# Three filter products and four tail-round blocks on Pool, with new orders of the filter stage and of the early inverse

## The chip, the cores and the metric

One core of a Trainium2 chip. The metric is the time of one execution on the device in microseconds (us); less is better. TensorE (PE) multiplies matrices and writes PSUM; VectorE (DVE), ScalarE (ACT) and GpSimd (POOL) do the element work; SyncE (SP) issues most transfers.

## The reference

`x` is 2048 x 576 in bfloat16.

```
h   = x + irfft2(rfft2(layernorm(x)) * (w_r + 1j*w_i))            # filter: 2048 x 289 complex weights
out = h + (gelu(layernorm(h) @ w_gate) * (layernorm(h) @ w_up)) @ w_down   # 576 -> 4608 -> 576
```

## The kernel before

The two-dimensional transforms are written as matmuls with tables. The kernel runs in stages: layer norm and a first transform over 128 rows (to about 20 us of the span), the **filter stage** (20 to 47 us), the **early inverse** with the second layer norm of the first six row tiles (47 to 58 us), and then the gated network in four blocks of 512 rows, 36 tiles of hidden columns each, every block followed by its down product. The inverse of the other ten row tiles is slipped into the first down product.

**Filter stage.** The 2048 row frequencies are cut into 16 groups i = 0..15. Each group goes through steps that are written as words, and the stage is a list of such words, `SEQF` (line 29). A word is a letter, a group and, if need be, an engine: `A` ACT (the default for evacuations), `D` DVE, `P` POOL, `x` for "directly from PSUM".

- `D i` and `d i` (`st_D`, line 621; matmuls on L628): the transform over columns, six matmuls in `D`, four in `d`, and then an evacuation of 128x576 from PSUM to the SBUF tile CUS.
- `B q` (`st_B`, line 635; L641): 16 matmuls, for groups 2q and 2q+1, which need both groups' CUS.
- `b i` (`ev_B`, line 644): evacuation of 128x576 from PSUM to YS, which has two buffers, i mod 2. With `x` there is none.
- `T i` (`st_T`, line 649; L653): the filter product, 128x1152, of YS (or, with `x`, of PSUM) with the weights WS in SBUF, into TP. On DVE before.
- `V i` (`st_V`, line 655; L661): 16 matmuls back from TP, and an evacuation of 128x512 to V.
- `Z i` (`st_Z`, line 666): copies the last 32 columns of each part of TP, 128x128, to ZR, where up to four groups lie beside one another.
- `R q` (`st_R`, line 670; L676 and L680): the **tail rounds**, eight matmuls over the four groups in ZR, and two products on DVE that spread the result with a mask MK into its block form VR. R0 serves group 0, R1 to R3 four groups each, R4 three.

All plain evacuations and copies go through one helper, `ev` (line 617), and so show as line L618. The program keeps the order of the words on each engine: an engine works its own words in the order of the list, and waits for others by semaphores. PSUM has eight banks, used as four pairs; `take` (line 600) gives a `D`, a `V`, an `R` or one of the two groups of a `B` the pair that was free for longest. A matmul that gets a used pair waits for the evacuation of what lay there. POOL operations wait for the POOL operation before.

**Early inverse.** `SEQ` (line 30) is a second list of words: `I` inverse over columns (L761; the first matmuls read V, the last VR), `N` inverse over rows and the residual add on DVE (L804, L821), `s` or `S` the squares for the layer norm on ACT or DVE, `q` and `c` root and reciprocal, `n` and `e` the scaling on DVE and POOL, `z` and `D` the transposes, `g` and `h` the first tiles of the gate and up products, for half of the rows each.

Of the kernel before, what the change touches and what calls it, by code (L numbers as in the profile page):

```python
# [4 lines left out]
BF16 = mybir.dt.bfloat16  # L5
F32 = mybir.dt.float32
ACTF = mybir.ActivationFunctionType
ALU = mybir.AluOpType
# [4 lines left out]
NP = 6  # L13
# [12 lines left out]
LORD = "x0-2 x2-4 a0-4 x4-8 a4-8 x8-12 x12-16 a8-16".split()  # L26
SPLIT = tuple(int(w[1:-1]) for w in SEQ1 if w[0] == "F")
ACT_TILES = tuple(int(w[1:]) for w in SEQ1 if w[0] == "Q")
SEQF = """D1 D0 d1D d0 D3 D2 d3 B0 b0 b1D T1 d2 D4 T0 d4 D5 B1 D6 b2 d5 b3D d6 T3 Z0D V1 Z1P T2 B2 D7 b4 D8 b5 d7D d8 T4 V3 V0 B3 T5 b6 b7 V2 D10 Z2P Z3D Z4D D9 d10 d9 T6 D11 T7 Z5P R0 d11 R1 B4 D13 Z6P b8 T8 b9 Z7D d13 T9 B5 D12 b10 b11 Z8D V4D V5 d12 Z9P T10 R2 D14 D15 d14 V9 d15 Z10P B6 T11 b13D b12 V7 V6 T13 V8 B7 T12 b15 V10 b14x T14x Z11P V11 T15 Z12P V12 V13 Z13P Z14P R3 V14 V15 Z15P R4""".split()
SEQ = """I0 I1 N0 I2 N1 s0 I3 S1 N2 q0 c0 I4 n0 s2 e0 q1 N3 e1 n1 I5 c1 z0 s3 e2 n2 D1 N4 q2 c2 D2 n3 N5 g10 e3 g00 h10 z3 h00 g20 g11 h20 h11 g01 g21 h01 h21""".split()  # L30
QR0 = ((0, 2), (2, 3), (3, 4))
QR = QR0 + ((4, NPRE), (NPRE, 8), (8, 16))
DSTEP, DLAG, ALAG = 288 // (16 - NPRE), 24, 26
# [293 lines left out]
def _build(nc, A_x, A_w_r, A_w_i, B_w_gate, B_w_up, B_w_down, out):  # L327
    P = Prog(nc)
    T = build_tables()
    dram = {n: nc.inline_tensor(_np_bf16(T[n]), name="c_" + n.lower()) for n in T}  # L330
    PE, DVE, ACT, SP, POOL = "pe", "dve", "act", "sp", "pool"
# [3 lines left out]
    sb = SbufMap(nc, base, top)  # L335
# [12 lines left out]
    V = sb.alloc("V", [128, 4, NT, NG, 8], BF16)  # L348
    VR = sb.alloc("VR", [128, NT, 2, NG, 8], BF16)
# [27 lines left out]
    MK = sb.alloc("MK", [128, 4], F32)  # L377
# [30 lines left out]
    TP = sb.alloc("TP", [128, NP, 2, 2, KW], BF16)  # L408
    ZR = sb.alloc("ZR", [128, 3, 4, 4, 32], BF16)
    GS = sb.alloc("GS", [128, 2, 2, KW], BF16)  # L410
    sb.off = v_off
    AT = sb.alloc("AT", [128, 36, 512], BF16)
    HT1 = sb.alloc("HT1", [128, 5, 512], BF16)
# [6 lines left out]
    PS = nc.alloc_psum_tensor("PS", [128, 4096], F32)  # L420

    def bank(b, p0=0, p1=128, c0=0, c1=512):
        return PS[p0:p1, b * 512 + c0:b * 512 + c1]

    def banks(b, n, w):
        return PS[:, b * 512:(b + n) * 512].rearrange("p (a c) -> p a c", a=n)[:, :, 0:w]
# [20 lines left out]
    for i, w in enumerate(LORD):  # L447
        c0, c1 = (int(v) for v in w[1:].rstrip("@").split("-"))
# [4 lines left out]
    WP = ((0, 4), (4, 10), (10, 16))  # L453
# [19 lines left out]
    wkeys = [[("W", pl, j, i) for pl in range(2) for i in range(6 if j else 7)] for j in range(3)]  # L473
# [106 lines left out]
    for w in SEQ1:  # L580
        a = w[1:]
# [4 lines left out]
    while c < NT:  # L586
        c1 = c + 1
        while c not in ACT_TILES and c1 < NT and c1 not in ACT_TILES:
            c1 += 1
        src, f, keys = (SA[:, 0, c:c1], -1.0 / D, "SA0") if c in ACT_TILES else (MV1[:, c:c1, 0], -1.0, "MV1")  # L590
        P.op(POOL, lambda g, c=c, c1=c1, src=src, f=f: g.tensor_scalar(NM[:, c:c1], src, f, 1.0, op0=ALU.mult, op1=ALU.mult),
             r=[(keys, k) for k in range(c, c1)], w=[("NM", k) for k in range(c, c1)])
# [5 lines left out]
    FB, used, held = {}, [0] * 4, {}  # L598
# [5 lines left out]

    for t, w in enumerate(SEQF):
        k, i, a = w[0], int(w[1:].rstrip("ADPx")), w[-1]
# [10 lines left out]
    def ev(eng, dst, src, r, w):  # L617
        fn = (lambda v: v.tensor_copy(dst, src)) if eng != ACT else (lambda a: a.activation(dst, src, ACTF.Copy))  # L618
        P.op(eng, fn, r=r, w=w)

    def st_D(i, second=False, eng=ACT):
        b0, s3 = FB["D", i], i % 4
        for j in range(3 - second):
            for half in range(2):
                o = half ^ second
                us, h0, b = (1 - o, 3 - o, 4)[j], 64 * half, b0 + o
                aft = [d_done[i, o]] if second and j == 0 else []
                d_done[i, o] = P.op(PE, lambda t, b=b, us=us, h0=h0, o=o, s=(not second and j == 0), e=(second and j == 1): t.matmul(  # L628
                    bank(b, 0, 128, 0, 2 * HK), U[h0:h0 + 64, us, i, :, :, :].rearrange("p s n e -> p (s n e)"), FT[h0:h0 + 64, 4 if us == 4 else 2 * o + us // 2, :], start=s, stop=e),
                    r=[("U", q, us, i // 8) for q in range(len(GROUPS))] + ["FT"], w=[("PS", b)], after=aft)  # L630
        if second:
            ev(eng, CUS[:, s3, :, :].rearrange("p a (j r) -> p a j r", r=2), banks(b0, 2, 2 * HK).rearrange("p r (a j) -> p a j r", a=2),
               [("PS", b0), ("PS", b0 + 1)], [("CU", s3)])
# [12 lines left out]
        if eng is not None:  # L646
            ev(eng, YS[:, i % 2, :, :], banks(b0, 2, KW), [("PS", b0), ("PS", b0 + 1)], [("Y", i % 2)])

    def st_T(i, direct=False):
        w4 = WS[:, :, i, 1:K2].unsqueeze(1).to_broadcast([128, 2, 2, KW])  # L650
        y, rk = (banks(FB["B", i], 2, KW), [("PS", FB["B", i] + h) for h in range(2)]) if direct else (YS[:, i % 2, :, :], [("Y", i % 2)])
        y4 = y.unsqueeze(2).to_broadcast([128, 2, 2, KW])
        P.op(DVE, lambda v: v.tensor_tensor(TP[:, i % NP, :, :, :], y4, w4, op=ALU.mult), r=rk + wkeys[sum(i >= w[1] for w in WP)], w=[("T", i % NP)])  # L653

    def st_V(i, b, eng):
        sp_ = int(i == 0)
# [10 lines left out]
        q, j = ((i - 1) // 4 % 2, (i - 1) % 4) if i else (2, 0)  # L667
        ev(eng, ZR[:, q, :, j, :], TP[:, i % NP, :, :, 256:KW].rearrange("p h w k -> p (h w) k"), [("T", i % NP)], [("ZR", q, j)])

    def st_R(q, b):  # L670
        j0, j1 = (4 * q - 3, min(4 * q + 1, NG)) if q else (0, 1)
        n, sp_, zb = j1 - j0, int(q == 0), (q - 1) % 2 if q else 2
        for k in range(4):
            for h in range(2):
                h0, vt = 64 * h, (0, 1, 1, 2)[k]
                P.op(PE, lambda t, k=k, h=h, h0=h0, vt=vt: t.matmul(bank(b + h, 0, 128, 0, 128), ZR[h0:h0 + 64, zb, k, :, :].rearrange("p a k -> p (a k)"),  # L676
                                                                    VT[h0:h0 + 64, sp_, vt, :].rearrange("p (k n e) -> p n k e", k=2, n=16), start=(k == 0), stop=(k == 3)),
                     r=[("ZR", zb, j) for j in range(4)] + ["VT"], w=[("PS", b + h)])
        for h in range(2):
            P.op(DVE, lambda v, h=h: v.tensor_tensor(VR[:, :, :, j0:j1, 4 * h:4 * h + 4].rearrange("p n k g e -> p (n k) g e"),  # L680
                                                     bank(b + h, 0, 128, 0, 128).rearrange("p (a e) -> p a e", e=4).unsqueeze(2).to_broadcast([128, 32, n, 4]),
                                                     MK[:, 0:n].unsqueeze(1).unsqueeze(3).to_broadcast([128, 32, n, 4]), op=ALU.mult),
                 r=[("PS", b + h), "MK"], w=[("V", g, 2) for g in range(j0, j1)])

    def idle_ft(n, b):
        for _ in range(n):
# [3 lines left out]
    d_done = {}  # L690
    for w in SEQF:
        i, e = int(w[1:].rstrip("ADPx")), {"A": ACT, "D": DVE, "P": POOL, "x": None}.get(w[-1], ACT)
        if w[0] == "D":
            st_D(i)
        elif w[0] == "d":
            st_D(i, True, e)
        elif w[0] == "B":
            st_B(i)
        elif w[0] == "b":
            ev_B(i, e)  # L700
        elif w[0] == "T":
            st_T(i, w[-1] == "x")
        elif w[0] == "Z":
            st_Z(i, e)
        elif w[0] == "V":
            st_V(i, FB["V", i], e)
        elif w[0] == "R":
            st_R(i, FB["R", i])


    wdv = B_w_down[:, :].rearrange("(c p) d -> p c d", p=128)
# [30 lines left out]

    MT = [int(w[1:]) for w in SEQ if w[0] == "M"]
    SLOT, last = {}, [0] * 4
    held = {}
    for t, w in enumerate(SEQ):
        k, i = w[0], int(w[1:])
        if k in "IJNMADzg":
            b = min((b for b in range(4) if b not in held), key=lambda b: last[b])
# [14 lines left out]
    def i_ev(c, eng=ACT):  # L764
        sl, b0 = c % 2, SLOT["I", c]
        if c == 0:
            P.op(DVE, lambda v, sl=sl, b0=b0: v.tensor_copy(GS[:, sl, 0, 0:KW], bank(b0, 0, 128, 0, KW)), r=[("PS", b0)], w=[("G", sl, 0)])
            P.op(ACT, lambda a, sl=sl, b0=b0: a.activation(GS[:, sl, 1, 0:KW], bank(b0 + 1, 0, 128, 0, KW), ACTF.Copy), r=[("PS", b0 + 1)], w=[("G", sl, 1)])
        else:
            ev(eng, GS[:, sl, :, 0:KW], banks(b0, 2, KW), [("PS", b0), ("PS", b0 + 1)], [("G", sl, 0), ("G", sl, 1)])  # L770

# [26 lines left out]
    def st_N(c):  # L798
        sl = c % 2
        for h in range(2):  # L800
            b = SLOT["N", c] + h
            for i in range(2):
                rhs = GS[:, sl, i, ::-1] if h else GS[:, sl, i, :]
                P.op(PE, lambda t, b=b, h=h, i=i, c=c, rhs=rhs: t.matmul(bank(b, 0, 128, 0, 288), IT[:, h * i, c, :], rhs, start=(i == 0 and c not in MT), stop=(i == 1)),  # L804
# [147 lines left out]

    gu_early = sorted({int(w[1]) for w in SEQ if w[0] == "g"})
    assert gu_early == list(range(len(gu_early)))
# [6 lines left out]
    st_I01()  # L961
    for w in SEQ[2:]:
        RUN[w[0]](int(w[1:]))
# [4 lines left out]


    fdead = ["DT", "IT", "J0", "J1", "ZD"] + [(n_, c) for n_ in ("ATB", "ATS") for c in range(NT)] + [("G", 0, 0), ("G", 0, 1), ("G", 1, 0), ("G", 1, 1), ("Y", 0), ("Y", 1)]  # L970
    fdead += [("T", a) for a in range(NP)] + [("ZR", a, h) for a in range(2) for h in range(4)]
    fnew = ([("AT", f) for f in range(36) if f not in gu_early] + [("GL", 0), ("GL", 1)] + [("HT", 1, i, k) for i in range(4) for k in range(5)])


# [5 lines left out]
    for j, c in enumerate(DEFS):  # L980
        b = 4 + 2 * (c % 2)
# [92 lines left out]
```

## Time and profile before

| | us |
|---|---|
| median of 3 runs | 489.96 (489.91 to 490.04) |
| the profiled execution | 489.97 |
| its span, first to last instruction | 487.7 |
| filter stage's matmuls, first to last | 20.47 to 46.01 |
| first matmul of the inverse that reads VR | 47.24 |
| gate and up matmuls without a break from | 57.74 |

| one instruction | engine | mean us | count |
|---|---|---|---|
| T from SBUF, 128x1152 | DVE | 0.755 | 15 |
| T from PSUM, 128x1152 | DVE | 1.349 | 1 |
| evacuation of 128x576 (d, b) | ACT | 0.65 | 26 |
| evacuation of 128x576 (d, b) | DVE | 0.758 | 5 |
| evacuation of V, 128x512 | ACT | 0.612 | 15 |
| VR half of R0, 128x128 | DVE | 0.292 | 2 |
| VR half of R1 to R3, 128x512 | DVE | 0.688 | 6 |
| VR half of R4, 128x384 | DVE | 0.558 | 2 |
| Z copy, 128x128 | DVE | 0.187 | 5 |
| Z copy, 128x128 | POOL | 0.42 (0.29 to 0.76) | 11 |

All durations are from the one profiled execution; consecutive instructions of an engine overlap by some 0.1 us, so that a row of evacuations on ACT goes at 0.55 us each. Matmuls are pipelined: the mean duration of a matmul in the profile is more than what it adds to a row of them.

### The profile page before, as it was taken

To read this page: it belongs to the slowest core of one execution; us is meant where nothing else is said; L and a number is where in the kernel's file an instruction comes from. 1 tells how busy PE (TensorE), PEld (TensorE's weight loads), DVE (VectorE), ACT (ScalarE), POOL (GpSimd) and SP (SyncE) were. 2 spreads that over 40 slices of the span, in tenths; PEclk is the share of its full clock that TensorE was granted. 3 is DMA by queue.
4 is the path that set the end of the run, shared out by engine and by line. 5 is a ranking of instruction groups with operands and counts; after the bars stand their busy time and mean duration, and the time that the engine had idled before them with its cause. 6 is when DMAs were issued, how large, how long until landed. Compare 5 with 4: busy or idle time off the path is not lost.

```text
span 487.7 us, 10651 instructions
## 1 busy us (share of the span) xinstructions
PE 479.9 (98%) x4725; PEld 281.8 (58%) x4726; DVE 191.6 (39%) x382; ACT 147.0 (30%) x289; POOL 33.8 (7%) x66
## 2 busy tenths in 40 slices
PE   7899999999999999999999999999999999999998
PEld 3667744444688744444577644444677444444775
DVE  6888733433576534333311144333211233333111
ACT  6898733223222222233200022332100123323000
POOL 5412720000000010000000000000000000000000
DMA  8657999300001071100000001000000000000000
GB/s 281 156 146 223 316 354 370 103 13 1 1 22 38 16 234 23 23 1 1 0 19 20 13 21 23 13 1 1 7 19 18 7 1 1 1 1 1 13 18 19
DMA packets 26205, 31.03 MB, mean 64 GB/s; under 512 B 11792, under 2 KB 18320, under 8 KB 26160
## 3 DMA queue, kind: packets, MB, share of 16 engines
q1 hardware_dynamic: 23904, 21.07, 15.1%
q0 software_dynamic: 2256, 9.29, 5.4%
q8 instruction: 37, 0.61, 0.5%
q14 instruction: 8, 0.07, 0.0%
HBM read 26.02 MB, written 2.36 MB: 58 GB/s over the span
## 4 chain that ended last, share of the span: by engine, by line
PE 94%; DVE 3%; DMA 1%; POOL 0%; issue 0%; SPq 0%; ACT 0%; POOLq 0%; DVEq 0%
PE PS L902 57%; PE PS L1003 29%; PE PS L628 2%; PE PS L661 1%; DVE ST L496 1%; DMA XO<-in_A_x_dram 1%; PE PS L920 1%; PE PS L641 1%; DVE VR L680 1%; PE PS L938 1%; DVE XO L821 0%; PE PS L804 0%; PE PS L761 0%; DVE ATS L527 0%; SPq L237 0%
## 5 line engine op out<-in xcount | busy, mean ns | idle before, releaser
L902 PE MATMUL PS<-HT,WG 64*128 64x512 bf16 (+1 forms) x2160 | 228.7, 371 | 0.0
L902 PEld LDWEIGHTS PS<-HT,WG 64*128 64x128 bf16 x2160 | 105.0, 94 | 122.0 <-issue 0.9
L911 DVE TENSOR_TENSOR AT<-GL,PS 128x512 bf16<-128x512 bf16 (+1 forms) x147 | 99.4, 677 | 177.9 <-ACT GL L910 177.9
L910 ACT ACTIVATE GL<-PS 128x512 bf16<-128x512 f32 (+1 forms) x147 | 86.5, 588 | 262.9 <-PE PS L902 251.6
L1003 PE MATMUL PS<-WD,AT 128*128 128x288 bf16 (+2 forms) x1152 | 144.9, 286 | 0.0
L1003 PEld LDWEIGHTS PS<-WD,AT 128*128 128x128 bf16 x1152 | 110.7, 98 | 30.6 <-ACT GL L910 1.3
L902 PE MATMUL PS<-HT,WGX 64*128 64x512 bf16 x486 | 53.4, 376 | 0.0
L1006 DVE TENSOR_TENSOR OS<-PS,XO 128x288 bf16<-128x288 f32 (+2 forms) x32 | 14.6, 457 | 94.4 <-PE PS L1003 94.3
L902 PEld LDWEIGHTS PS<-HT,WGX 64*128 64x128 bf16 x486 | 23.7, 94 | 28.8
L628 PE MATMUL PS<-FT,U 64*128 64x288 bf16 x160 | 12.1, 284 | 0.4 <-ACT U L564 0.3
L925 ACT ACTIVATE EB<-PS 128x288 f32<-128x288 f32 x10 | 4.1, 410 | 27.7 <-PE PS L920 27.7
L553 PE MATMUL PS<-ATS,XO 128*128 128x128 bf16 x96 | 9.1, 220 | 2.6 <-POOL ATS L522 2.1
L653 DVE TENSOR_TENSOR TP<-YS,WS 128x1152 bf16<-128x1152 bf16 x15 | 11.0, 755 | 0.4 <-ACT YS L618 0.2
L496 DVE BATCH_NORM_STATS2 ST<-XO 128x6 f32<-128x288 bf16 x26 | 9.9, 441 | 2.3 <-DMA XO<-in_A_x_dram 2.3
L943 DVE TENSOR_TENSOR XO<-PS,XO 128x576 bf16<-128x576 f32 x10 | 7.6, 757 | 8.0 <-PE PS L938 8.0
L553 PEld LDWEIGHTS PS<-ATS,XO 128*128 128x128 bf16 x96 | 6.8, 98 | 4.9 <-POOL ATS L522 3.3
L931 DVE TENSOR_TENSOR QB<-PS,EB 128x288 f32<-128x288 f32 x20 | 8.2, 452 | 3.3 <-ACT EB L925 3.3
L848 DVE TENSOR_SCALAR HN<-XO,NM,RS 128x576 bf16<-128x576 bf16 (+1 forms) x28 | 9.3, 368 | 0.0
L564 ACT ACTIVATE U<-PS 128x384 bf16<-128x384 f32 (+2 forms) x29 | 9.2, 415 | 0.1
L618 ACT ACTIVATE CUS<-PS 128x576 bf16<-128x576 f32 x14 | 8.8, 657 | 1.4 <-PE PS L628 1.4
L628 PEld LDWEIGHTS PS<-FT,U 64*128 64x128 bf16 x160 | 6.4, 94 | 4.2 <-PE PS L628 0.7
L661 PE MATMUL PS<-VT,TP 64*128 64x128 bf16 x256 | 8.7, 217 | 0.1
(86 smaller groups left out, 203.1 us busy)
## 6 DMA issues: line engine op xcount, KB each, us to landing
WD<-in_B_w_down_dram POOLq DMA_DIRECT2D x9, 576.0 KB, 17.1
WG<-in_B_w_up_dram SPq DMA_DIRECT2D x3, 1152.0 KB, 12.7
WG<-in_B_w_gate_dram POOLq DMA_DIRECT2D x2, 1152.0 KB, 13.1
out_dram<-OS SPq DMA_DIRECT2D x30, 72.0 KB, 1.6
XO<-in_A_x_dram SPq DMA_DIRECT2D x3, 576.0 KB, 7.1
WG<-in_B_w_gate_dram SPq DMA_DIRECT2D x4, 288.0 KB, 3.8
WG<-in_B_w_up_dram SPq DMA_DIRECT2D x4, 288.0 KB, 3.7
WG<-in_B_w_gate_dram SPq DMA_DIRECT2D x1, 1152.0 KB, 9.6
```

The source lines that it names most:

```text
L496: P.op(DVE, lambda v: v.bn_stats(ST1[:, c, h, :], XO[:, c, 288 * h:288 * h + 288]), r=[("X", c)], w=[("ST1", c, h)])
L553: P.op(PE, lambda t, b=b, lhs=lhs, s=s, e=e, o=o, c=c: t.matmul(bank(b, 0, 128, o, o + 128), lhs, ATS[:, c, :], start=s, stop=e), r=[("X", ...
L564: fn = (lambda v: v.tensor_copy(dst, src)) if eng == DVE else (lambda a: a.activation(dst, src, ACTF.Copy))
L628: d_done[i, o] = P.op(PE, lambda t, b=b, us=us, h0=h0, o=o, s=(not second and j == 0), e=(second and j == 1): t.matmul(bank(b, 0, 128, 0, ...
L653: P.op(DVE, lambda v: v.tensor_tensor(TP[:, i % NP, :, :, :], y4, w4, op=ALU.mult), r=rk + wkeys[sum(i >= w[1] for w in WP)], w=[("T", i % ...
L661: P.op(PE, lambda t, c=c, h0=h0, h=h, k=k, vt=vt: t.matmul(bank(b + h, 0, 128, 128 * c, 128 * c + 128), TP[h0:h0 + 64, i % NP, k // 2, k % ...
L848: P.op(eng, lambda v, c=c, hs=hs, o0=o0, o1=o1, x0=x0, x1=x1: v.tensor_scalar(HN[:, hs, o0:o1], XO[:, c, x0:x1], NM[:, c:c + 1], RS2[:, c: ...
L902: op = P.op(PE, lambda t, h0=h0, kt=kt, wt=wt, b=b, s=(not second and j == 0), e=(second and j == n - 1): t.matmul(bank(b, 0, 128, c0, c1) ...
L910: P.op(ACT, lambda a: a.activation(GL[:, s2, c0:c1], bank(b0, 0, 128, c0, c1), ACTF.Gelu_apprx_tanh), r=[("PS", b0)], w=[("GL", s2)])
L911: P.op(DVE, lambda v: v.tensor_tensor(AT[:, f, c0:c1], GL[:, s2, c0:c1], bank(b0 + 1, 0, 128, c0, c1), op=ALU.mult), r=[("GL", s2), ("PS", ...
L1003: P.op(PE, lambda t, b=b, d0=d0, d1=d1, f=f, p=p: t.matmul(bank(b, 0, 128, 0, d1 - d0), AT[:, f, 128 * p:128 * p + 128], WD[:, f, d0:d1], ...
L1006: P.op(DVE, lambda v, b=b, d0=d0, d1=d1, p=p, c=c: v.tensor_tensor(OS[:, p % 2, d0:d1], bank(b, 0, 128, 0, d1 - d0), XO[:, c, d0:d1], op=A ...
```

## The change

A product `T iP` runs on POOL (T1, T7 and T12). For `R qP` (R0 to R3), ACT first copies the result of the eight matmuls from PSUM to a new SBUF tile RD, 128x256 in bfloat16, and the two products that make VR then run on POOL. R4 stays on DVE. Three products read PSUM directly, where it was one (T3, T8 and T14, before T14). Both lists of words are new; in `SEQF` the engine of many evacuations and copies changes too: `d` 11 on ACT and 5 on DVE (before 14 and 2), `b` 8 and 5 (before 12 and 3), `V` 14 and 2 (before 15 and 1), `Z` 6 on ACT, 5 on DVE and 5 on POOL (before none, 5 and 11). The matmuls are the same in number and shape.

```diff
-SEQF = """D1 D0 d1D d0 D3 D2 d3 B0 b0 b1D T1 d2 D4 T0 d4 D5 B1 D6 b2 d5 b3D d6 T3 Z0D V1 Z1P T2 B2 D7 b4 D8 b5 d7D d8 T4 V3 V0 B3 T5 b6 b7 V2 D10 Z2P Z3D Z4D D9 d10 d9 T6 D11 T7 Z5P R0 d11 R1 B4 D13 Z6P b8 T8 b9 Z7D d13 T9 B5 D12 b10 b11 Z8D V4D V5 d12 Z9P T10 R2 D14 D15 d14 V9 d15 Z10P B6 T11 b13D b12 V7 V6 T13 V8 B7 T12 b15 V10 b14x T14x Z11P V11 T15 Z12P V12 V13 Z13P Z14P R3 V14 V15 Z15P R4""".split()
-SEQ = """I0 I1 N0 I2 N1 s0 I3 S1 N2 q0 c0 I4 n0 s2 e0 q1 N3 e1 n1 I5 c1 z0 s3 e2 n2 D1 N4 q2 c2 D2 n3 N5 g10 e3 g00 h10 z3 h00 g20 g11 h20 h11 g01 g21 h01 h21""".split()
+SEQF = """D0 D1 D2 d0D d1 D3 d2 d3D B0 b1 b0D T1P D4 d4 T0 B1 b3x b2 T3x Z0 Z1P D5 T2 D6 d5 D7 d6 d7D B2 b4 V1 b5D V3 V0 V2 B3 T4 T5 D8 D9 Z2 Z3 b6D b7 d8 Z4D d9D T6 D10 T7P Z5P R0P d10 D11 R1P d11 B4 b8x b9 Z6D T8x Z7D D12 V4 T9 d12 D14 B5 Z8 b10 b11D Z9 D13 d14 d13D D15 T10 R2P d15 Z10D V5 B6 b12 T11 V7 b13D V6 T13 V8 B7 b15 T12P V9 b14x T14x Z11D T15 Z12P V10 Z13P V11 V13D Z14P R3P V12D Z15 V15 V14 R4""".split()
+SEQ = """I0 I1 N0 I2 N1 S1 s0 I3 N2 q0 I4 c0 n1 n0 e0 e1 N3 s2 q1 c1 I5 D1 s3 n2 z0 q2 N5 c2 N4 n3 e2 D2 g10 g00 e3 h10 z3 h00 g20 g01 h20 g11 h01 g21 h11 h21""".split()
...
+    RD = sb.alloc("RD", [128, 2, 2, 128], BF16)
...
-    def st_T(i, direct=False):
+    def st_T(i, direct=False, eng=DVE):
...
-        P.op(DVE, lambda v: v.tensor_tensor(TP[:, i % NP, :, :, :], y4, w4, op=ALU.mult), r=rk + wkeys[sum(i >= w[1] for w in WP)], w=[("T", i % NP)])
+        P.op(eng, lambda v: v.tensor_tensor(TP[:, i % NP, :, :, :], y4, w4, op=ALU.mult), r=rk + wkeys[sum(i >= w[1] for w in WP)], w=[("T", i % NP)])
...
-    def st_R(q, b):
+    def st_R(q, b, eng=DVE):
...
+        if eng == POOL:
+            ev(ACT, RD[:, q % 2, :, :], banks(b, 2, 128), [("PS", b), ("PS", b + 1)], [("RD", q % 2, 0), ("RD", q % 2, 1)])
         for h in range(2):
-            P.op(DVE, lambda v, h=h: v.tensor_tensor(VR[:, :, :, j0:j1, 4 * h:4 * h + 4].rearrange("p n k g e -> p (n k) g e"),
-                                                     bank(b + h, 0, 128, 0, 128).rearrange("p (a e) -> p a e", e=4).unsqueeze(2).to_broadcast([128, 32, n, 4]),
-                                                     MK[:, 0:n].unsqueeze(1).unsqueeze(3).to_broadcast([128, 32, n, 4]), op=ALU.mult),
-                 r=[("PS", b + h), "MK"], w=[("V", g, 2) for g in range(j0, j1)])
+            src, key = (RD[:, q % 2, h, :], ("RD", q % 2, h)) if eng == POOL else (bank(b + h, 0, 128, 0, 128), ("PS", b + h))
+            P.op(eng, lambda v, h=h, src=src: v.tensor_tensor(VR[:, :, :, j0:j1, 4 * h:4 * h + 4].rearrange("p n k g e -> p (n k) g e"),
+                                                              src.rearrange("p (a e) -> p a e", e=4).unsqueeze(2).to_broadcast([128, 32, n, 4]),
+                                                              MK[:, 0:n].unsqueeze(1).unsqueeze(3).to_broadcast([128, 32, n, 4]), op=ALU.mult),
+                 r=[key, "MK"], w=[("V", g, 2) for g in range(j0, j1)])
...
-            st_T(i, w[-1] == "x")
+            st_T(i, w[-1] == "x", POOL if e == POOL else DVE)
...
-            st_R(i, FB["R", i])
+            st_R(i, FB["R", i], POOL if e == POOL else DVE)
```

More of the change, by code (lines that the diff above doesn't have):

```diff
@@ L970, in _build @@
     fdead = ["DT", "IT", "J0", "J1", "ZD"] + [(n_, c) for n_ in ("ATB", "ATS") for c in range(NT)] + [("G", 0, 0), ("G", 0, 1), ("G", 1, 0), ("G", 1, 1), ("Y", 0), ("Y", 1)]
-    fdead += [("T", a) for a in range(NP)] + [("ZR", a, h) for a in range(2) for h in range(4)]
+    fdead += [("T", a) for a in range(NP)] + [("ZR", a, h) for a in range(2) for h in range(4)] + [("RD", a, h) for a in range(2) for h in range(2)]
     fnew = ([("AT", f) for f in range(36) if f not in gu_early] + [("GL", 0), ("GL", 1)] + [("HT", 1, i, k) for i in range(4) for k in range(5)])
```

## The prediction

> **What bounds the kernel now.** I read the table of engines, the chain that ended last, the same chain in order of time, and busy time by stage.
>
> ```profile
> PE 94%; DVE 3%; DMA 1%; POOL 0%; issue 0%; SPq 0%; ACT 0%; POOLq 0%; DVEq 0%
> ```
>
> TensorE carries the whole span, so time can be won only where it idles. The change touches two stages: the filter stage (20.44 to 47.20 us) and the early inverse (47.20 to 57.70); from 57.7 us on PE is busy all the time. Busy time in these two windows (columns: window, length, PE, weight load, DVE, ACT, POOL, clock, DMA):
>
> ```profile
> 20.44:47.20 26.76, 26.00 (x589) 18.65 (x589) 22.85 (x40) 23.46 (x45) 4.62 (x11) 1.00 0.64 178
> 47.20:57.70 10.50, 10.11 (x105) 7.55 (x107) 8.36 (x19) 8.49 (x19) 5.94 (x10) 1.00 0.94 299
> ```
>
> PE, DVE and ACT are all nearly full in the filter stage; POOL has over 20 us free. Pipelined matmuls count as busy, so I add PE's real work from the chain in order of time: a D opening 0.36 us (6 matmuls), its second half 0.24, a B 0.61, a V 0.46, an R 0.24. 16 x 0.60 + 8 x 0.61 + 16 x 0.46 + 5 x 0.24 = 23.1 us. The stage's matmuls run from 20.47 to 46.01 (R4's end): 2.4 us idle. Then the tail of the chain:
>
> ```profile
> 42.45 1.95 PE PS L661 x64
> 44.40 0.27 PE PS L676 x8
> 44.67 0.69 DVE VR L680
> 45.36 0.02 issue
> 45.38 1.21 DVE VR L680 x2
> 46.60 0.02 issue
> 46.62 0.57 DVE VR L680
> 47.19 0.05 issue
> 47.24 1.03 PE PS L761 x7
> ```
>
> The inverse goes ahead at 47.24 when the last block of tail rounds (VR) is written. So the end of R4's VR is the stage's due time. The most that the stage can give is 2.4 us plus about 1 us of this tail.
>
> **The change, part by part.** Durations are the mean of one in the groups by shape.
>
> *Off DVE:* three products, 3 x 755 ns = 2.3 us; VR of R0 to R3, 2 x 292 + 6 x 688 = 4.7 us. *Onto DVE:* two more products read PSUM directly, 2 x 1349, in place of two at 755 (+1.2); five more evacuations of 576 columns, 5 x 758 = 3.8; one more V, 0.7. By kind DVE falls from 23.9 to 22.6 us.
> *ACT:* d from 14 to 11, b from 12 to 8 (7 fewer at about 0.655 = 4.6 off), V from 15 to 14 (0.6 off). On: six tail copies Z of 128 columns (nearest row: 128x192 at 343 ns; I take 0.3) and four copies of R to SBUF, 128x256 (between 343 for 192 columns and 410 for 288; 0.38). Net 26.2 to 24.3 us.
> *PE:* the same matmuls, 23.1 us.
> *POOL:* no row shows such a product on POOL. Nearest:
>
> ```profile
> L522 POOL TENSOR_TENSOR ATS<-ATB,RS 128x384 bf16<-128x384 bf16 x2 | 1.7, 827 | 0.7 <-DVE RS L517 0.6 <-POOL XN L569 0.2
> L522 POOL TENSOR_TENSOR ATS<-ATB,RS 128x256 bf16<-128x256 bf16 x1 | 0.6, 612 | 0.1
> ```
>
> Two sizes give 1.68 ns per element and a base of 0.18 us. A product of 1152 elements: 2.12 us; a VR half of 512: 1.04, of 128: 0.40. POOL goes from 4.6 to 3 x 2.12 + 6 x 1.04 + 2 x 0.40 + 5 x 0.42 = 15.5 us. Bounds for the product: 1.15 us by the one-input rows (XN: 619 ns for 512, 831 for 768, 0.83 ns per element), 3 us above. I take 2.12, as the row is the same operation. The Trainium skill's page "GPSIMD Engine Reference", section 3.1, gives about 2.6 cycles per element for two inputs at 1.2 GHz; that would be an estimate of 2.7 us. No run here shows it.
>
> By sums alone the change relieves DVE and ACT by 1.3 and 1.9 us and could close most of the 2.4 us. What decides is whether POOL and DVE can work at once.
>
> **Do they?** The timeline of POOL and of DVE (start, us):
>
> ```profile
> 25.27 0.76 POOL L618 COPY ZR<-TP 128x128 bf16<-128x128 bf16 x1 [5.74 <-DVE TP L653]
> 28.20 0.29 POOL L618 COPY ZR<-TP 128x128 bf16<-128x128 bf16 x1 [2.17 <-DVE TP L653]
> ...
> 32.39 0.76 POOL L618 COPY ZR<-TP 128x128 bf16<-128x128 bf16 x1 [0.86 <-DVE TP L653]
> ```
>
> ```profile
> 24.45 1.43 DVE L653 TENSOR_TENSOR TP<-YS,WS 128x1152 bf16<-128x1152 bf16 x2
> ```
>
> The same copy takes 0.29 us alone and 0.76 when a DVE product from SBUF runs: it ends at 26.03, 0.15 after the products end (25.88). Beside the product that reads PSUM (42.54 to 43.89) the copies keep 0.29. So a product of two SBUF operands shuts POOL out. The other direction, DVE behind POOL:
>
> ```profile
> 16.32 0.50 DVE L527 TENSOR_SCALAR ATS<-ATB,RS 128x128 bf16<-128x128 bf16 x1
> ```
>
> The same scaling takes 0.25 us in the other seven cases. Here a POOL copy began 0.10 before it (16.22) and ended at 16.77; DVE ended 0.05 later. Whoever is first keeps the other out. But at 54.10 a DVE scaling that began 0.01 after a POOL one was not delayed: POOL needs a lead of about 0.1 us. That a *product* on DVE is delayed by a *product* on POOL is not in the trace; it is inferred.
> The Trainium skill's page "SBUF — State Buffer", section "Who interferes with whom", says so outright: a DVE instruction with two SBUF inputs and a GpSimd instruction that reads SBUF exclude each other for the whole instruction. By that rule the stalls below are real; without it the sum would be the first rival's.
>
> **Walk of the new order.** Evacuations start 0.25 us after the last matmul of a D, 0.11 after a B, 0.33 after a V; PE goes on 0.2 after an evacuation; back to back, ACT takes 0.55 (V 0.49) and DVE 0.67 to 0.7.
> 1. *Opening.* D0 D1 D2 come before the first second half, so the first evacuation starts at 22.04, not 21.68; but two engines share the four, and B0 runs 23.15 to 23.76 (before: 22.79). b1 on ACT 23.87 to 24.52, b0 on DVE 23.9 to 24.66. T1 on POOL starts at 24.58, T0 on DVE is ready at 24.79: POOL leads by 0.2 us. T1 ends at 26.7; T0 runs 26.5 to 27.25. b2 (ACT) overwrites the buffer T0 reads, so it waits until 27.3 (before: 25.91). Behind b2 in ACT's queue stand Z0, d5, d6; PE needs b2's bank for D7, which starts at 28.15. V1 begins at 29.85 after 6.6 us of PE work: 2.75 us idle. Before, at 30.10, it was 1.0 after 8.6 us. Cost: 1.7 us.
> 2. *Middle.* T7 on POOL (33.8 to 35.95) holds T6 until 35.75, but T6 has slack; R1's pair (37.6 to 40.3) meets T9. PE reaches B6 at 41.4 with 4.2 us idle; before, at like work, 2.1. Cost so far: 2.1.
> 3. *End.* R2's pair (41.4 to 44.2) delays T11 to 42.4 and T13 to 44.0; T12 on POOL then gets its turn only at 44.75 to 46.85 and holds T15 until 46.65. Z12, Z13, Z14 and R3 queue behind T12 on POOL: R3's pair ends at 50.6, R4's VR at about 50.9, against 47.19. Cost in all: 3.5 us.
> The walk charges every wait in full, with the product at 2.12. At 1.15 us each of the two products on the path (T1, T12) costs 1 us less: 1.6 us in all. At 3 us it is 5. I take +2.7, between the first two.
> 4. *Early inverse.* Its order swaps neighbours (second square ahead, n1 before n0, N5 before N4); PE idles about 1 us in it. I take -0.2, bounds -0.6 and +0.4.
> 5. *DMA.* POOL's weight loads, issued at 49.19, stand behind R3's products and go about 1.5 us later; they land in some 13 us and are first needed after nine gate tiles of 1.95 us, at 75 us. SP's loads wait for PE's 601st matmul, near 41 us; they land about 50, the gate matmuls start at 55.7. Nothing.
>
> The profiled execution took 489.97 us with a span of 487.7; the median is 489.96. 489.97 + 2.7 - 0.2 = **492.5 us**.
>
> **Rivals.**
> *A. DVE isn't held by POOL, or the products are placed so that they don't meet.* Same walk without the stalls: T0 at 24.8, b2 at 25.5, D7 at 26.3, B6 at 39.4, R4's end about 45.5, VR at 46.7 or earlier. -0.5 from that, up to -1.5 if all idle but 1 us goes, and -0.2 from the inverse: 488.0 to 489.5, centre 489.0. For it: the sums, and no product seen delayed. Against: the 0.50 us row.
> *B. T0 wins the race with T1P.* It needs 0.1 to 0.2 us of my estimates to be wrong. T0 runs 24.8 to 25.5, T1 25.5 to 27.6, still before V1. The opening costs nothing; the end's meeting of R2, T11, T13 and T12 stays, about half of it: +0.6, 489.8 to 491.4.
> *C. The slower side further out.* POOL's product near 3 us, by which T12 alone comes a microsecond later and R3 ends last: 494 to 495. It decides from about 2.5 us on.
>
> **How the numbers follow.** Forecast (DVE held, POOL first) 0.50, own range 491.3 to 494.0; A 0.27; B 0.17; C 0.06. A change within 0.2% (1.0 us) is about what a measurement can't tell from none: of A 0.07 and of B 0.10 lie there, so faster 0.20, same 0.17, slower 0.63. The range leaves out a tenth below and a tenth above: 488.7 to 494.0.
>
> **What would show it.** The groups by shape: the SBUF product on DVE over 755 ns on the mean, single ones 1.5 to 2.7 us; the product on POOL near 2.1 us. The timeline: T1 on POOL ahead of T0, and an ACT wait of over 1 us for it near 25 us; D7 at 28 instead of 26. The last VR, then the inverse, at 49 to 51 rather than 47.24. I am wrong if DVE's products stay at 755 ns, or if they stretch only where PE has other work.

## The result and the profile after

The changed kernel takes 493.78 us (median of 5 runs, 493.62 to 493.85), against 489.94 before (5 runs): a ratio of 1.0078, 95% interval 1.0063 to 1.0093. It is 3.8 us slower. The forecast was 492.5, with a range of 488.7 to 494.0, so the time lies 0.2 under the range's upper end. Times here and below are medians over executions; in one kernel below, t_pool, two of four executions had a granted TensorE clock of 0.997 where every other one had 1.000, and were 1.5 us longer, so only its other two are used.

The profiled execution took 493.85 us with a span of 492.1. The chain that ended last, by engine:

```profile
PE 90%; DVE 6%; DMA 1%; POOL 1%; issue 1%; ACT 0%; SPq 0%; POOLq 0%; DVEq 0%
```

PE has lost four points of the chain, DVE has gained three and POOL one: the end is now set for some 15 us more by DVE. Where that is, the busy times of the two stages tell (window, length, PE, weight load, DVE, ACT, POOL, clock, DMA). The first window goes from the first filter matmul to the first inverse matmul on VR, the second on to the unbroken gate stage:

```profile
20.59:51.50 30.91, 25.96 (x589) 18.93 (x590) 27.18 (x35) 22.12 (x47) 18.17 (x17) 1.00 0.55 165
51.50:62.08 10.58, 10.07 (x105) 7.69 (x107) 8.20 (x19) 8.43 (x19) 5.72 (x10) 1.00 0.95 324
```

The filter stage has grown from 26.8 to 30.9 us and the early inverse has stayed (10.50 before, 10.58 now). PE is busy for as long as before. DVE, from which three products and four tail rounds were taken, is busy for 27.2 us where it was 22.9. The groups by shape say with what (line, engine, operation, count, busy us, mean ns):

```profile
L654 DVE TENSOR_TENSOR TP<-YS,WS 128x1152 bf16<-128x1152 bf16 x10 | 10.8, 1084 | 0.2
L654 DVE TENSOR_TENSOR TP<-PS,WS 128x1152 bf16<-128x1152 f32 x3 | 4.0, 1349 | 0.0
...
L619 DVE COPY ZR<-TP 128x128 bf16<-128x128 bf16 x5 | 3.1, 626 | 0.1
```

The same product of two SBUF operands went from 755 to 1084 ns on the mean, and the tail copy on DVE from 187 to 626. The product that reads PSUM is what it was (1349). So the longer time isn't in more work (by kind DVE has 1.3 us less, as the prediction added up); some instructions take longer. It is few of them: two of the ten products (2.71 and 2.12 us) and three of the five copies (0.84 to 0.99). The list of waits shows no wait of DVE for it: an instruction that is kept out of SBUF is recorded as running, with T0 at 2.71 us, not as waiting. The views of the opening, POOL, DVE, ACT and PE in order of time:

```profile
24.83 2.12 POOL L654 TENSOR_TENSOR TP<-YS,WS 128x1152 bf16<-128x1152 bf16 x1 [5.16 <-ACT YS L619]
```

```profile
24.85 2.71 DVE L654 TENSOR_TENSOR TP<-YS,WS 128x1152 bf16<-128x1152 bf16 x1
27.49 1.35 DVE L654 TENSOR_TENSOR TP<-PS,WS 128x1152 bf16<-128x1152 f32 x1
```

```profile
24.87 0.65 ACT L619 ACTIVATE CUS<-PS 128x576 bf16<-128x576 f32 x1 [0.27 <-PE PS L629]
27.60 0.65 ACT L619 ACTIVATE YS<-PS 128x576 bf16<-128x576 f32 x1 [2.08 <-DVE TP L654]
```

```profile
28.30 1.03 PE L629 MATMUL PS<-FT,U 64*128 64x288 bf16 x14 [1.77 <-ACT YS L619]
```

POOL's T1 starts 0.02 us ahead of DVE's T0. T0, an instruction of 0.755 us, lasts 2.71 and ends 0.62 after T1. The evacuation b2 on ACT then sits 2.08 us for T0's buffer, and PE, which needs b2's bank, is idle for 1.77. The second long product is T6, beside T7 on POOL:

```profile
33.66 2.37 POOL L654 TENSOR_TENSOR TP<-YS,WS 128x1152 bf16<-128x1152 bf16 x1 [5.94 <-ACT YS L619]
```

```profile
34.52 2.12 DVE L654 TENSOR_TENSOR TP<-YS,WS 128x1152 bf16<-128x1152 bf16 x1
```

It too ends 0.61 after POOL's product. At the other end of the stage the chain in order of time:

```profile
46.22 0.84 DVE ZR L619
47.07 0.67 DVE TP L654
47.73 0.61 DVE V L619
48.34 0.30 POOL ZR L619
...
48.76 0.30 POOL ZR L619
...
49.20 1.04 POOL VR L684
...
50.33 1.04 POOL VR L684
51.37 0.14 issue
51.51 1.02 PE PS L765 x7
```

The inverse goes ahead at 51.51 (47.24 before), after R3's second half on POOL; R4's, on DVE, was done at 51.17.

### The profile page after: what moved, and what is told of

The parts are those of the page before. It is cut to its first block, busy times and chain, and to the rows that moved or that the text cites. A ratio compares the mean times of both kernels' runs of the same rounds, so it can differ in the third digit from the quotient of the medians.

```text
span 492.1 us, 10651 instructions
## 1 busy us (share of the span) xinstructions
PE 480.2 (98%) x4726; PEld 282.6 (57%) x4726; DVE 196.0 (40%) x377; ACT 145.6 (30%) x291; POOL 47.1 (10%) x71
## 4 chain that ended last, share of the span: by engine, by line
PE 90%; DVE 6%; DMA 1%; POOL 1%; issue 1%; ACT 0%; SPq 0%; POOLq 0%; DVEq 0%
PE PS L906 57%; PE PS L1007 29%; DVE TP L654 2%; DVE ST L497 1%; DMA XO<-in_A_x_dram 1%; PE PS L924 1%; PE PS L629 1%; PE PS L942 0%; DVE ZR L619 0%; DVE CUS L619 0%; PE PS L808 0%; POOL VR L684 0%; PE PS L662 0%; PE PS L765 0%; DVE YS L619 0%
## 5 line engine op out<-in xcount | busy, mean ns | idle before, releaser
L654 DVE TENSOR_TENSOR TP<-YS,WS 128x1152 bf16<-128x1152 bf16 x10 | 10.8, 1084 | 0.2
L539 PE MATMUL PS<-ZD 128*128 128x512 bf16 x20 | 7.7, 552 | 1.5 <-POOL ZD L431 1.5
## 6 DMA issues: line engine op xcount, KB each, us to landing
WD<-in_B_w_down_dram POOLq DMA_DIRECT2D x9, 576.0 KB, 15.2
```

Of the source, the lines that this page charges most:

```text
L654: P.op(eng, lambda v: v.tensor_tensor(TP[:, i % NP, :, :, :], y4, w4, op=ALU.mult), r=rk + wkeys[sum(i >= w[1] for w in WP)], w=[("T", i % ...
```

## The experiments

The theory: POOL's reads of SBUF and DVE's instructions with two SBUF operands, or its SBUF copies, shut each other out, whoever is first. The rivals: POOL is just slow and its queue sets the end; the detour of R over ACT and SBUF is what costs; the new orders are bad (or good) by themselves. Ten kernels were run. All times are medians beside the kernel before on the same chip (489.91 to 489.96).

**memset: POOL as long, but reading nothing.** Each product on POOL is replaced by memsets of about the same length. The three filter products and four tail blocks are left out. The code is shortened here:

```diff
+        if eng == POOL:
+            for _ in range(2):
+                P.op(POOL, lambda v: v.memset(TP[...], 0.0), r=(as the product), w=[("T", i % NP)])
+            return
...
+            if eng == POOL:
+                for _ in range(2 if n > 1 else 1):
+                    P.op(POOL, lambda v, h=h: v.memset(VR[...], 0.0), r=[("RD", q % 2, h), "MK"], w=(as the product))
+                continue
```

> All of the change, with each product on POOL replaced by POOL memsets of about the same length (two of 1152 elements for a filter product, two of 512 or one of 128 for a VR half); three filter products and four tail-round blocks are left out so. A memset writes the same tile after the same waits but reads nothing from SBUF. Theory (POOL's reads of SBUF keep DVE's SBUF products and copies out): every SBUF product on DVE takes 0.755 us again, T0 too (2.71 in the changed kernel), the evacuation behind it starts near 25.7 instead of 27.6, the inverse at 46.3 to 47.8 instead of 51.5; time 488.8 to 490.3. Rival (POOL is simply a slow engine, and its queue or the new order sets the end): POOL's chain keeps its length, so the time stays within 0.7 of 493.8.

Measured: 489.39 us, ratio 0.9988 (0.9978 to 0.9998). POOL and DVE of this run in order of time, the opening:

```profile
24.71 1.06 POOL L656 MEMSET TP<- 128x1152 bf16 x1 [5.13 <-ACT YS L619]
```

```profile
24.75 0.76 DVE L658 TENSOR_TENSOR TP<-YS,WS 128x1152 bf16<-128x1152 bf16 x1
```

The groups by shape:

```profile
L658 DVE TENSOR_TENSOR TP<-YS,WS 128x1152 bf16<-128x1152 bf16 x10 | 7.5, 755 | 0.2
L619 DVE COPY ZR<-TP 128x128 bf16<-128x128 bf16 x5 | 1.9, 387 | 0.1
```

POOL again leads, by 0.04 us, and writes the same tile, yet T0 takes 0.76, and all ten products are back at 755 ns. The inverse goes ahead at 47.06. The two memsets take 2.17 us together, as long as the product, so the theory holds against a slow POOL: 4.4 us hang on POOL's *reading*. That is both directions at once, as POOL's queue is shorter here too: the memsets keep their length beside DVE (1.06 and 0.53 us on the mean), and POOL is busy for some 3 us less of the stage (15.2 against 18.2). One thing stayed long: three of the five tail copies on DVE (0.55, 0.58 and 0.43 us). The first of them, beside a memset that ends at 33.76:

```profile
33.27 0.55 DVE L619 COPY ZR<-TP 128x128 bf16<-128x128 bf16 x1
```

It ends 0.05 us after the memset and takes 0.55 instead of 0.19: a DVE copy is kept out by a POOL instruction that only writes. The Trainium skill's page "SBUF — State Buffer", section "Who interferes with whom", makes this distinction: a DVE instruction with two SBUF inputs contends with a GpSimd instruction that reads SBUF and not with one that only writes it, while a DVE instruction in a 2-port mode, which copies can enter, contends with GpSimd in any case. Both trace rows agree; that this copy runs in such a mode is not shown by them.

**t1_after_t0 and t0_direct: the opening by itself.** One lets T1 on POOL wait for T0; the other lets T0 read PSUM.

```diff
-... b0D T1P D4 d4 T0 B1 ...
+... b0D T0 T1P D4 d4 B1 ...        # t1_after_t0; T1 also reads ("T", 0)
```

```diff
-... B0 b1 b0D T1P D4 d4 T0 B1 ...
+... B0 b1 b0x T1P D4 d4 T0x B1 ... # t0_direct
```

> The change with one wait more: POOL's T1 also waits for DVE's T0, so that T0 gets the port first. Theory: T0 takes 0.755 us, the evacuation b2 starts near 25.7 and D7 near 26.6 instead of 28.3; T1 ends near 27.8, before its V. 1.6 us are won in the opening, and the later meetings give a part back: 492.0 to 493.0. Rival (T1 is late because POOL is slow): T1 comes 0.8 later, so 493.8 to 494.6.

> The change with one word pair more: b0 and T0 become b0x and T0x, so T0 reads PSUM and not YS, beside T1 on POOL. Theory: T0 has one SBUF operand and takes 1.35 us beside POOL's T1 (2.71 in the changed kernel), T1 keeps 2.1, the evacuation b2 needn't wait for T0 and starts near 25.7; 1.5 to 2 us are won in the opening: 491.7 to 492.7. Rival (any DVE product is slowed beside POOL, whatever it reads): T0 over 2 us, 493.3 to 494.

Measured: 492.24 us (ratio 1.0046, 1.0031 to 1.0061) and 491.91 us (1.0041, 1.0027 to 1.0055), so 1.5 and 1.9 us better than the change. DVE in t1_after_t0, in order of time:

```profile
24.82 0.76 DVE L654 TENSOR_TENSOR TP<-YS,WS 128x1152 bf16<-128x1152 bf16 x1
25.50 1.35 DVE L654 TENSOR_TENSOR TP<-PS,WS 128x1152 bf16<-128x1152 f32 x1
26.77 1.69 DVE L654 TENSOR_TENSOR TP<-YS,WS 128x1152 bf16<-128x1152 bf16 x1
```

T0 is short again; T1 on POOL now runs from 25.72 to 27.84, and it is T2, begun at 26.77, that is held by it. That costs less: d7 stands behind T2 on DVE, and PE waits for it ahead of V3.

```profile
29.18 1.51 PE L662 MATMUL PS<-VT,TP 64*128 64x128 bf16 x48 [0.57 <-DVE CUS L619]
```

So PE waits 0.57 us here in place of 1.77, and B3 starts at 30.62 in place of 31.79: 1.2 of the 1.5 us are won in the opening, by what T0 no longer passes on to ACT and PE. In t0_direct, DVE and POOL:

```profile
23.90 1.36 DVE L654 TENSOR_TENSOR TP<-PS,WS 128x1152 bf16<-128x1152 f32 x1
25.41 1.36 DVE L654 TENSOR_TENSOR TP<-PS,WS 128x1152 bf16<-128x1152 f32 x1 [0.16 <-PE PS L642]
```

```profile
24.72 2.12 POOL L654 TENSOR_TENSOR TP<-YS,WS 128x1152 bf16<-128x1152 bf16 x1 [5.15 <-ACT YS L619]
```

T0 (23.90) no longer waits for an evacuation, starts 0.8 us ahead of T1 and lies beside it for only 0.54 us, so its 1.36 us says little about products from PSUM. T3 (25.41) says it: it reads PSUM, lies wholly inside T1 here and mostly inside it in t1_after_t0, and takes 1.36 and 1.35 us, and T1 keeps 2.12.

**orders, t_pool, r_pool: the parts one by one.** In the changed kernel's word lists the `P` is taken off both kinds of product, off the four R alone, or off the three T alone.

```diff
-... T1P ... T7P ... R0P ... R1P ... R2P ... T12P ... R3P ...
+... T1  ... T7  ... R0  ... R1  ... R2  ... T12  ... R3  ...   # orders
+... T1P ... T7P ... R0  ... R1  ... R2  ... T12P ... R3  ...   # t_pool
+... T1  ... T7  ... R0P ... R1P ... R2P ... T12  ... R3P ...   # r_pool
```

> The new orders alone: T1, T7, T12 and R0 to R3 all back on DVE. Theory: nothing on POOL but five copies, so every SBUF product takes 0.755 us, but DVE has about 27 us to do back to back from 22.1 us on, and the inverse begins at 50 to 51.5: 492.5 to 494.0. Rival (the new orders are good by themselves, POOL's part spoils them): 489.0 to 490.5.

> New orders, the three filter products on POOL, but R0 to R3 back on DVE from PSUM. Theory: the blocks behind T1, T7 and T12 stay, DVE's tail copies fall from 0.8 to 1.0 us to 0.19, and DVE gets 4.8 us more work: 492.5 to 494.5. Rival (the detour of R costs): 490.0 to 491.5.

> New orders, R0 to R3 on POOL, but the three filter products T1, T7 and T12 back on DVE. Theory: no block of 2 us is left, T0 takes 0.755 us, R3 no longer stands behind T12 on POOL; DVE has 2.2 us more to do and 3.3 us less to wait: 490.3 to 492.0. Rival (the detour of R over ACT, SBUF and POOL is what costs): 493.0 to 494.0.

| new orders, us | R0 to R3 on DVE | R0 to R3 on POOL |
|---|---|---|
| T1, T7, T12 on DVE | orders 493.73 (ratio 1.0064 to 1.0092) | r_pool 490.99 (1.0012 to 1.0030) |
| T1, T7, T12 on POOL | t_pool 495.85 (495.80 and 495.89) | the change 493.78 (1.0063 to 1.0093) |

In these orders, R on POOL saves 2.7 us with T on DVE and 2.1 us with T on POOL; T on POOL costs 2.1 us with R on DVE and 2.8 us with R on POOL. So each part has its sign with or without the other, but together they are 0.7 us worse than their sum. That R3 stands behind T12 in POOL's queue fits this; it was not tried by itself. The orders alone are slow for another reason: DVE's instructions all keep their length there, but the new list gives DVE 5.7 us more to do (1.2 in direct products, 3.8 in evacuations, 0.7 in V), and it is nearly full. From 20.50 to 51.30 (the first inverse matmul on VR), and the product in the groups:

```profile
20.50:51.30 30.80, 27.11 (x589) 19.03 (x590) 27.87 (x46) 21.27 (x43) 5.38 (x9) 1.00 0.54 156
```

```profile
L654 DVE TENSOR_TENSOR TP<-YS,WS 128x1152 bf16<-128x1152 bf16 x13 | 9.5, 755 | 0.0
```

DVE is busy for 27.9 of 30.8 us, near the expected 27. The change's DVE is busy for 27.2, only 0.7 less: it got rid of 7 us of own work (three products and the VR of R0 to R3), and took back 10 x 0.33 + 5 x 0.44 = 5.5 us in stretched products and copies (means of 1084 against 755, and 626 against 187). That is where most of the relief went; these sums count the overlap of neighbours twice and so don't close to the tenth.

t_pool missed its range (492.5 to 494.5): it is the slowest of all. The late part of its chain goes through T12 on POOL:

```profile
46.11 2.69 POOL L654 TENSOR_TENSOR TP<-YS,WS 128x1152 bf16<-128x1152 bf16 x1 [9.51 <-PE PS L662]
48.86 0.80 POOL L619 COPY ZR<-TP 128x128 bf16<-128x128 bf16 x1
```

With R on DVE the matmuls come later, T12 waits for the one that frees its buffer, starts 1.6 us later than in the change, and R3 with R4 queue on DVE behind it. I had added the loads and not followed the buffer.

**new_inv: the early inverse alone.** The kernel before, with the second list of words from the change.

> The kernel before with the change's order of the early inverse alone. From the first matmul on VR to the unbroken gate stage it was 10.50 us before and 10.57 after, so the theory is no difference: 489.9 to 490.2. Rival (the new order saves 0.2 us, as predicted): 489.6 to 489.8.

Measured: 490.03 us, ratio 1.0003 (0.9994 to 1.0012): no difference.

**old_r012, old_r12 and r_pool_za: is there a version that beats both?** R on POOL helped in the new orders, so it was tried in the old ones (both lists as before, `R0P R1P R2P`, then `R1P R2P` only); and r_pool with the old second list and DVE's five tail copies moved to ACT (`Z4D Z6D Z7D Z10D Z11D` to `Z4 Z6 Z7 Z10 Z11`).

> Both orders of the kernel before, with R0, R1 and R2 alone made by POOL from SBUF copies; all filter products on DVE. Theory: DVE loses 3.3 us of work and ACT gains 1.1, and the pairs of POOL (1.04 us a half) meet DVE's products where DVE is nearly full, about 1 us of stall each for R1 and R2; the net is near nothing: 489.3 to 490.6. Rival (R on POOL is worth 2.7 us wherever it is, as between the new orders alone and these with R on POOL): 487.5 to 488.7.

> As old_r012, but R0 stays on DVE: R1 and R2 on POOL. Theory: 0.3 us apart from old_r012 at most. Rival: within 0.3 us of old_r012 too; the run is there to see a version that beats the kernel before, if one of the two does.

> New filter order with R0 to R3 on POOL and all filter products on DVE, the five tail copies of DVE moved to ACT, and the old order of the inverse. Theory: the copies' 0.37 us (0.185 alone) leave DVE, so 490.0 to 490.8 against 490.99. Rival (ACT is as full as DVE): 491.0 to 491.8.

Measured: 491.10 (ratio 1.0023, 1.0014 to 1.0032), 490.57 (1.0013, 1.0004 to 1.0022) and 490.19 us (1.0004, 0.9995 to 1.0013). The first is outside both ranges, the second 0.5 better than the first where at most 0.3 was expected. In old_r012, DVE's groups:

```profile
L654 DVE TENSOR_TENSOR TP<-YS,WS 128x1152 bf16<-128x1152 bf16 x15 | 11.6, 799 | 2.7 <-ACT YS L619 2.5
L619 DVE COPY ZR<-TP 128x128 bf16<-128x128 bf16 x5 | 1.8, 372 | 0.0
```

The first line of these is of the products, the second of the tail copies. DVE has room now, but stands idle for 2.5 us in front of its products, waiting for ACT's evacuations (0.2 in the kernel before), and ACT got the copies to RD on top. One DVE copy takes 1.03 us behind R1. Of the 2.5 us, 2.34 are one wait in front of T8, where in the kernel before the VR of R0 and R1 stood:

```profile
35.44 1.35 DVE L654 TENSOR_TENSOR TP<-YS,WS 128x1152 bf16<-128x1152 bf16 x1 [2.34 <-ACT YS L619]
```

```profile
33.24 1.94 DVE L680 TENSOR_TENSOR VR<-PS,MK 128x128 bf16<-128x128 f32 x4 [0.25 <-PE PS L676]
```

T8 started at 35.10 then, so at this place taking R0 and R1 off DVE freed time that nothing used. This fits a gain of 2.7 us that is a gain only where DVE has few such gaps, as in the new orders; it was not tried further. r_pool_za did what was expected, 0.8 us better than r_pool, and is level with the kernel before. No version here beats it.

## Why the prediction was right, point by point

- *What bounds the stage.* Right: PE's work is the same, the time moved with the last VR.
- *The price on POOL.* Right: 2.12 us expected for the product; T1, which nothing held up, took 2.115. T12 took 2.50, begun while T13 ran on DVE; T7 took 2.37, though DVE was idle when it began (33.44 to 33.85), and why is not shown. R3's halves of 512 took 1.04 (1.04 expected), those of R1 and R2 beside DVE's products and copies up to 1.54 (mean of the six 1.24), a half of 128 0.40; the copies to RD 0.38 (0.38), a tail copy on ACT 0.30 to 0.34 (0.3). The estimate of 2.7 us after the Trainium skill's page "GPSIMD Engine Reference", section 3.1, was too high for this operation, which took 2.115; the page's figure is from fp32.
- *DVE is held by POOL.* It was inferred from one row of 0.50 us in another stage; T0's 2.71 us, and 0.76 beside the memset, show it.
- *POOL needs a lead of about 0.1 us.* Wrong: a recorded 0.02 was enough at T0. I had 0.2 for the lead. The outcome was the one forecast, but by a margin that was not there, which is luck; rival B was nearer than its 0.17.
- *The walk.* Its times came out close: b2 at 27.60 (27.3 expected), D7 at 28.30 (28.15), V1 at 29.88 (29.85), B6 at 41.58 (41.4), T12 from 44.52 to 47.02 (44.75 to 46.85), T15 at 46.99 (46.65), R3's end at 51.36 (50.6), R4's at 51.17 (50.9). What it lacked: DVE's tail copies behind the first halves of R1 and R2 (0.99 and 0.91 us) and behind T12 (0.84), and a gap of 0.46 between POOL's copies Z12 and Z13, which the trace puts down to DVE's evacuation of V. "T6 has slack" was wrong: T6 is held until 36.64, lies on the chain that ended last, and PE waits 0.53 us at 38.19 for T8 behind it. So the middle came out close with a step in it that was wrong.
- *The size.* Too small, +2.5 in all against +3.8, and the mis-sized term is "I take +2.7": the walk had 3.5, and I shaded it toward the figure for a product of 1.15 us, for which no row of the same operation spoke. In the trace the filter stage cost 30.91 - 26.80 = 4.1 us, from 20.59 to 51.50 against 20.44 to 47.24.
- *Early inverse, -0.2.* Wrong in size: +0.08 in the trace, and no difference by itself (new_inv).
- *DMA, nothing.* Not contradicted; POOL's weight loads were issued at 51.30, 2.1 us later, and the gate stage ran without a break.
- *Rival A, 489.0 without the stalls.* The memset kernel comes near that case: 489.39, inside A's 488.0 to 489.5. The relief by sums was real, but without the stalls it was worth 0.6 us of the 2.4 us of idle time.

The spans differ by 4.4 us, the profiled times by 3.88. The time outside the span was 2.27 us before and 1.75 after; why that is shorter was not tried.

## What to carry to other kernels

Before work that is moved from DVE to POOL counts as relief, look at the DVE instructions beside it: here those that read PSUM kept their 1.35 us, those with two SBUF operands took up to 2.7 in place of 0.755, and tail copies up to 0.99 in place of 0.19. The move can still pay: R on POOL saved 2.7 us where DVE was nearly full. Before such a move, look in the old trace for one short instruction that is too long beside the other engine, and then walk the order by hand, with the buffer that each late instruction frees; here the walk's sum of 3.5 was nearer to the 3.8 than the cautious middle of 2.7. A stretched instruction doesn't appear among the waits: compare the mean of a shape with its undisturbed value.

## What the runs showed that was not expected

- A recorded lead of 0.02 us was enough for POOL's product to keep DVE's out for its whole length (24.83 against 24.85).
- POOL's memset of 128x1152 (1.06 us) left a DVE product of two SBUF operands alone, but stretched a DVE copy of 128x128 from 0.19 to 0.55 us; two more copies took 0.58 and 0.43 beside memsets.
- In the new orders one half of the move paid and the other did not: R on POOL saved 2.1 to 2.7 us, T on POOL cost 2.1 to 2.8 us.
